# Cached attention on one core: transposing P on TensorE as 4-byte pairs of keys

## The chip, the cores and the metric

The kernel runs on one core of a Trainium2 chip. Time is the device time of one execution in microseconds (us). Before the change the median of two runs is 958.55 us (958.49 to 958.61).

## The reference

Two independent attention blocks, A and B, have the same shapes; their outputs are laid side by side. All tensors are bfloat16.

```python
B, Sq, D = 16, 64, 640
H, Sk, Dh = 32, 512, 128
q = (x @ wq).reshape(B, Sq, H, Dh).transpose(0, 2, 1, 3)
scores = jnp.einsum("bhqd,bhkd->bhqk", q, k_cache) * (Dh ** -0.5)
p = softmax(scores, axis=-1)
o = jnp.einsum("bhqk,bhkd->bhqd", p, v_cache)
return o.transpose(0, 2, 1, 3).reshape(B, Sq, H * Dh) @ wo
```

The K and V caches are most of the data: 16 x 32 x 512 x 128 elements each, for each block.

## The kernel before

**Tiling.** The 64 queries of two batch rows are put together to fill 128 partitions. A *step* g is one head of one such pair of batch rows; a *macro-step* m, called an iteration below, is two steps. A *group* is a pair of batch rows with 16 heads (8 iterations), a *pass* is half the heads of one block with all 8 pairs of batch rows. There are 4 passes and 256 iterations. K and V come in chunks of 4 heads through rings of five buffers, loaded on SyncE's queue (SP).

**One iteration**, by the names in the program (line numbers are those of the profile):

- KX (L433, TensorE) transposes K of the two heads, one batch row at a time (KX0, KX1: eight transposes of 128x128 each), into the one PSUM bank KTB. KE (L442, VectorE) copies the bank to `ktp_ring`. K is loaded with `t=8`: partition pp holds keys 8pp to 8pp+7, and so the transposed keys, and the scores after them, lie in the order (t, pp): key 8pp+t stands at place 64t+pp.
- QP2 (L451, TensorE) projects q, QE2 (L459, ScalarE) copies it out.
- SM2 (L467, TensorE) computes the scores of both steps into two PSUM banks, one for each step.
- MX (L476, VectorE) takes the row maximum; EX (L482, ScalarE) writes exp(score - max) to `p_ring` in bfloat16 and sums it to `rowsum`; RC2 (L488, VectorE) is the reciprocal of two sums.
- NM (L496, POOL) multiplies by the reciprocal and, with a permuting access pattern, writes `pn_ring` in the order in which the transposes need the keys.
- TR2 (L505, TensorE) transposes the normalised P: four 128x128 transposes for each step, eight in all, into the PSUM bank PTB; TE2 (L512, VectorE) copies the bank to `pT_ring`.
- PV2 (L524, TensorE) multiplies by V, which is loaded with `t=4` (partition p holds keys 4p to 4p+3); OE2 (L532, ScalarE) copies the result out.
- OP2 (L540, L545, TensorE) multiplies by wo and accumulates over the 16 heads of a group. At the group's end OVP (L555, ScalarE) stores a partial sum or, in the second pass of a block, OVF (L560, VectorE) adds it and writes `out_sb`, and ST sends that to DRAM from ScalarE's queue. XT (L604) and XE (L612) transpose x for a later group once in each group.

**Order.** Each engine runs a fixed list, made from templates that say which iteration (an offset to k) each operation works on in round k:

```python
PE_T = (("TR2", 1), ("QP2", 4), ("KX", 4, 0), ("SM2", 3), ("PV2", 1), ("XT", 0), ("OP2", 0), ("KX", 4, 1))
ACT_T = (("QE2", 4), ("OE2", 1), ("XE", 0), ("EX", 3, 0), ("EX", 3, 1), ("OV", 0), ("ST", -1))
DVE_T = (("TE2", 1), ("RC2", 2), ("KE", 4, 0), ("MX", 3, 0), ("MX", 3, 1), ("KE", 4, 1), ("OVF", 0))
POOL_T = (("NM", 0, 0), ("NM", 0, 1))
```

So a round on TensorE is TR2, QP2, KX0, SM2, PV2, OP2, KX1. Within an engine the order never changes. Between engines, `build_plan` lists the reads and writes of each operation, derives the dependences and turns them into semaphore waits. The loads on SP are sorted by due time from planned durations.

Of the kernel before, what the change touches and what calls it, by code (L numbers as in the profile page):

```python
# [64 lines left out]
def build_plan(dims, cfg):  # L65
# [32 lines left out]
    def make_op(kind, m, sub):  # L98
        g0, g1 = 2 * m, 2 * m + 1
        ps_, bp, grp, h0 = step_info(g0)  # L100
        c = g0 // G
        if kind == "KX":
            return mk("pe", "KX", (m, sub), [("kn", c % cfg.NKB, g0 % G), ("kn", c % cfg.NKB, g1 % G), ("ident",)],
                      [("KTB",)], "KX%d" % sub, m, sub)
        if kind == "KE":
            return mk("dve", "KE", (m, sub), [], [("KTB",), ("ktp", m % cfg.NKT, sub)], "KE%d" % sub, m, sub)
        if kind in ("MX", "EX", "NM"):
            g = 2 * m + sub
            r = g % cfg.NR
            if kind == "MX":  # L110
                return mk("dve", "MX", g, [], [("SB", sub), ("negmax", r)], "MX%d" % sub, m, sub)
            if kind == "EX":
                return mk("act", "EX", g, [("negmax", r)], [("SB", sub), ("p", g % cfg.NP), ("rowsum", r)],
                          "EX%d" % sub, m, sub)
            return mk("pool", "NM", g, [("p", g % cfg.NP), ("recip", r)], [("pn", g % cfg.NPN)], "NM%d" % sub, m, sub)
        r0, r1 = g0 % cfg.NR, g1 % cfg.NR
        if kind in ("XT", "XE"):
            mt = m + cfg.XLEAD
            if mt % MPG != 0 or not (0 <= mt < NMAC):
                return None  # L120
            gq = mt // MPG
            m_ts = mt - cfg.XLEAD + OFF["TR2"]
            if kind == "XT":
                return mk("pe", "XT", gq, [("xn", gq % cfg.NXN), ("ident",)], [("PTB",)], "XT", m_ts, aux=gq)
            return mk("act", "XE", gq, [], [("PTB",), ("xT", gq % cfg.NX)], "XE", m_ts, aux=gq)
        if kind == "QP2":
            return mk("pe", "QP2", m, [("xT", grp % cfg.NX), ("wq", ps_ % 2, h0 // G)], [("QB",)], "QP2", m)
        if kind == "QE2":
            return mk("act", "QE2", m, [], [("QB",), ("qT", m % cfg.NQ)], "QE2", m)
        if kind == "SM2":  # L130
            return mk("pe", "SM2", m, [("qT", m % cfg.NQ), ("ktp", m % cfg.NKT, 0), ("ktp", m % cfg.NKT, 1)],
                      [("SB", 0), ("SB", 1)], "SM2", m)
        if kind == "RC2":
            return mk("dve", "RC2", m, [("rowsum", r0), ("rowsum", r1)], [("recip", r0), ("recip", r1)], "RC2", m)
        if kind == "TR2":
            return mk("pe", "TR2", m, [("pn", g0 % cfg.NPN), ("pn", g1 % cfg.NPN), ("ident",)], [("PTB",)], "TR2", m)
        if kind == "TE2":
            return mk("dve", "TE2", m, [], [("PTB",), ("pT", m % cfg.NT)], "TE2", m)
        if kind == "PV2":
            return mk("pe", "PV2", m, [("pT", m % cfg.NT), ("v", c % cfg.NVB, g0 % G), ("v", c % cfg.NVB, g1 % G)],  # L140
                      [("OB",)], "PV2", m)
        if kind == "OE2":
            return mk("act", "OE2", m, [], [("OB",), ("oT", m % cfg.NO)], "OE2", m)
        if kind == "OP2":
            return mk("pe", "OP2", m, [("oT", m % cfg.NO), ("wo", ps_ % 2, h0 // G)], [("OUTB",)], "OP2", m)
        if kind in ("OV", "OVF", "ST"):
            if h0 + 1 != SPB - 1:
                return None
            last_half = ps_ % NHALF == NHALF - 1
            if kind == "OV":  # L150
                if NHALF == 1:
                    return mk("act", "OV", m, [], [("OUTB",), ("out_sb", grp % 2)], "OV", m, aux=grp)
                if last_half:
                    return None
                return mk("act", "OVP", m, [], [("OUTB",), ("outp", bp)], "OV", m, aux=grp)
            if kind == "OVF":
                if NHALF == 1 or not last_half:
                    return None
                return mk("dve", "OVF", m, [("outp", bp)], [("OUTB",), ("out_sb", grp % 2)], "OV", m, aux=grp)
            if NHALF == 1 or not last_half:  # L160
                return None
            return mk("act", "ST", m, [("out_sb", grp % 2)], [("out_dram", grp)], "ST", m, aux=grp)
        raise ValueError(kind)

    templates = {"pe": cfg.PE_T, "dve": cfg.DVE_T, "pool": cfg.POOL_T, "act": cfg.ACT_T}
    for eng, tmpl in templates.items():
        offs = [t[1] for t in tmpl] + [cfg.XLEAD]
        for k in range(-max(offs), NMAC - min(offs)):
            for t in tmpl:
# [8 lines left out]
                if 0 <= m < NMAC:  # L178
                    op = make_op(kind, m, sub)
                    if op is not None:  # L180
                        progs[eng].append(op)
                        if op.kind == "OV":
                            progs[eng].append(mk("act", "ST", m, [("out_sb", op.aux % 2)], [("out_dram", op.aux)],
                                                 "ST", m, aux=op.aux))

    progs["pool"] = [mk("pool", "INIT1", -1, [], [("ones",)], "LDW", -10),
                     mk("pool", "INIT2", -1, [("ones",)], [("ident",)], "LDX", -10)] + progs["pool"]

    loads = []
    NEG = -10 ** 9  # L190
# [53 lines left out]
    def sem_key(op):  # L244
# [5 lines left out]
            return ("d_" + op.kind[2:].lower(), op.aux[0] % 2, op.aux[1])  # L250
        if op.kind == "ST":
            return ("d_out", op.aux % 2)
        if op.kind in ("INIT1", "INIT2"):
            return ("s_init",)
        return ("s_" + op.kind.lower(),)

# [90 lines left out]
def mha_kernel(nc, blocks, out, cfg=None):  # L347
# [30 lines left out]
    with contextlib.ExitStack() as es:  # L378
# [13 lines left out]
        qT_ring = sb("qT_ring", [128, NQ, 2, 128], BF16)  # L392
        p_ring = sb("p_ring", [128, NP, SK], BF16)
        pn_ring = sb("pn_ring", [128, NPN, SK], BF16)
        pT_ring = sb("pT_ring", [128, NT, 2, 4, 128], BF16)
        oT_ring = sb("oT_ring", [128, NO, 2, 128], BF16)
        out_sb = sb("out_sb", [128, 2, DN], BF16)
        negmax = sb("negmax", [128, NR], F32)
        rowsum = sb("rowsum", [128, NR], F32)
        recip = sb("recip", [128, NR], F32)  # L400
        ones_sb = sb("ones_sb", [128, 128], BF16)
        ident = sb("ident", [128, 128], BF16)
        ps = es.enter_context(nc.psum_tensor("ps", [128, 8, 512], F32))

        sems = {}
# [9 lines left out]
        S_BANK0 = 2  # L415
        PT_BANK, O_BANK, Q_BANK, KT_BANK = 4, 5, 6, 7
        pt_ps_flat = ps[:, PT_BANK, :].bitcast(BF16)
        pt_ps = pt_ps_flat.rearrange("p (s t q) -> p s t q", s=2, t=4)
        o_ps = ps[:, O_BANK, 0:256]
        q_ps = ps[:, Q_BANK, 0:256]  # L420
        kt_ps_flat = ps[:, KT_BANK, :].bitcast(BF16)
# [57 lines left out]
        def em_EX(e, op):  # L479
            g = op.idx  # L480
            r = g % NR
            ins = e.activation(p_ring[:, g % NP, :], s_bank(g % 2), ACTF.Exp, bias=negmax[:, r:r + 1], scale=1.0,  # L482
                               accum_out=rowsum[:, r:r + 1])
            return ins, ins

# [5 lines left out]
        def em_NM(e, op):  # L491
            g = op.idx
            r = g % NR
            src = p_ring[:, g % NP, :].rearrange("q (th tl pp) -> q th tl pp", th=2, tl=4)
            dst = pn_ring[:, g % NPN, :].rearrange("q (tl pp th) -> q th tl pp", tl=4, th=2)
            ins = e.tensor_scalar(dst, src, recip[:, r:r + 1], 1.0, ALU.mult, ALU.mult)  # L496
            return ins, ins

        def em_TR2(e, op):
            m = op.idx  # L500
            first = last = None
            for sub in range(2):
                g = 2 * m + sub
                for t in range(4):
                    ins = e.transpose(pt_ps[:, sub, t, :], pn_ring[:, g % NPN, t * 128:(t + 1) * 128], ident[:, :])  # L505
                    first = first or ins
                    last = ins
            return first, last

        def em_TE2(e, op):  # L510
            m = op.idx
            ins = e.tensor_copy(pT_ring[:, m % NT].rearrange("p s t q -> p (s t q)"), pt_ps_flat)  # L512
            return ins, ins

        def em_PV2(e, op):
            m = op.idx
            first = last = None
            for sub in range(2):
                g = 2 * m + sub
                c, gi = g // G, g % G  # L520
                for j in range(2):
                    for t in range(4):
                        col = sub * 128 + 64 * j
                        ins = e.matmul(o_ps[:, col:col + 64], v_ring[:, c % NVB, j, gi, t, :],  # L524
                                       pT_ring[:, m % NT, sub, t, 64 * j:64 * j + 64], start=(t == 0), stop=(t == 3))
                        first = first or ins
                        last = ins
            return first, last
# [18 lines left out]
            return first, last  # L547

        def em_OV(e, op):
            ins = e.activation(out_sb[:, op.aux % 2, :], out_ps_all, ACTF.Copy)  # L550
            return ins, ins

        def em_OVP(e, op):
# [3 lines left out]

        def em_OVF(e, op):
            blk, bp = grp_info(op.aux)
            ins = e.tensor_tensor(out_sb[:, op.aux % 2, :], out_ps_all, outp[:, bp, :], ALU.add)  # L560
            return ins, ins

        def em_ST(e, op):
            blk, bp = grp_info(op.aux)
            dst = out[2 * bp:2 * bp + 2, :, blk * DN:(blk + 1) * DN].rearrange("b q n -> (b q) n")
            ins = e.dma_start(dst, out_sb[:, op.aux % 2, :])
            return ins, ins

        def em_INIT1(e, op):
# [2 lines left out]

        def em_INIT2(e, op):
            ins = e.affine_select(ident[:, :], ones_sb[:, :], [[1, 128]], ALU.is_equal, 0.0, base=0,
                                  channel_multiplier=-1)
            return ins, ins

# [38 lines left out]
        def em_LDKV(e, op):  # L616
# [6 lines left out]
            else:  # L623
# [4 lines left out]

        emitters = dict(KX=em_KX, KE=em_KE, QP2=em_QP2, QE2=em_QE2, SM2=em_SM2, MX=em_MX, EX=em_EX, RC2=em_RC2,
                        NM=em_NM, TR2=em_TR2, TE2=em_TE2, PV2=em_PV2, OE2=em_OE2, OP2=em_OP2, OV=em_OV,  # L630
                        OVP=em_OVP, OVF=em_OVF, ST=em_ST, XT=em_XT, XE=em_XE, INIT1=em_INIT1, INIT2=em_INIT2,
                        LDWQ=em_LDWQ, LDWO=em_LDWO, LDX=em_LDX, LDK=em_LDKV, LDV=em_LDKV)

        def run_program(e, prog, final_waits=()):
# [85 lines left out]
```

## Time and profile before

| What | Value |
|---|---|
| median of the runs | 958.55 us |
| profiled execution, span from first to last instruction | 956.8 us |
| TensorE busy | 919.4 us (96%) |
| VectorE busy | 841.9 us (88%) |
| ScalarE busy | 567.1 us (59%) |
| POOL busy | 416.9 us (44%) |
| DMA | 299.51 MB, mean 313 GB/s |
| mean granted TensorE clock | 0.998 |

The profiled execution is one of its own; its span is 1.75 us below the median of the timed runs. Busy time of TensorE counts each matmul with its latency, and neighbours overlap: the time of a burst is read from its first start to its last end, or from the chain of waits. In the groups of the page, the number after the busy time is the mean duration of one instruction in ns; what follows the second bar is the idle time of the engine just before the group's instructions, and what ended it. PEld are the weight loads of TensorE. In the timeline the columns are start, duration, engine, line, operation, output and inputs, and how many instructions are merged in the row.

### The profile page before, as it was taken

The numbers are of one execution on the slowest core, as the hardware profiler recorded it, in microseconds if no ns is written. First come the engines' busy times: TensorE is split into PE (matmuls) and PEld (weight loads), VectorE is DVE, ScalarE is ACT, GpSimd is POOL, SyncE is SP. The second block draws the span as 40 slices with busy tenths as digits, with TensorE's granted clock in tenths as the row PEclk, the third lists the DMA queues.
The fourth block names the chain that finished last, engine by engine and source line by source line (L and its number), as shares of the span: only waits on it lengthen the run. The fifth ranks groups of instructions, "written<-read, shape, count | busy, mean of one in ns | idle before, by whom it ended". The sixth has DMA issues, their size and how long they took to land.

```text
span 956.8 us, 34351 instructions
## 1 busy us (share of the span) xinstructions
PE 919.4 (96%) x14755; PEld 733.5 (77%) x15008; DVE 841.9 (88%) x1552; ACT 567.1 (59%) x1585; POOL 416.9 (44%) x518
## 2 busy tenths in 40 slices
PE   4999999999999999999999999999999999999997
PEld 3877777778777777877777787777877778777775
DVE  2898899898899999899999899889899998999996
ACT  1666656666665565656566666666666656565654
POOL 0444444444444444444444444444444444444443
PEclk9999999999999999999999999999999999999999
DMA  9999999999999999888999999988888988899830
GB/s 315 364 365 364 351 365 367 365 368 351 338 337 337 343 330 315 299 292 305 322 332 352 326 353 327 306 294 296 302 305 288 308 301 297 295 297 314 295 124 15
DMA packets 230871, 299.51 MB, mean 313 GB/s; under 512 B 9536, under 2 KB 165184, under 8 KB 230720
## 3 DMA queue, kind: packets, MB, share of 16 engines
q1 hardware_dynamic: 228416, 294.69, 91.0%
q8 instruction: 118, 1.93, 0.8%
q10 hardware_dynamic: 2304, 2.62, 0.8%
q14 instruction: 33, 0.27, 0.1%
HBM read 294.65 MB, written 2.62 MB: 311 GB/s over the span
## 4 chain that ended last, share of the span: by engine, by line
PE 89%; DVE 4%; POOL 3%; issue 2%; SPq 1%; DMA 1%; POOLq 0%; DVEq 0%
PE ps L433 22%; PE ps L524 14%; PE ps L451 14%; PE ps L467 14%; PE ps L505 12%; PE ps L545 7%; PE ps L540 5%; POOL pn_ring L496 3%; DVE out_sb L560 1%; DVE ktp_ring L442 1%; DVE pT_ring L512 1%; PE ps L604 1%; DMA xn_ring<-in_A_x_dram 1%; SPq L626 1%; SPq L583 1%
## 5 line engine op out<-in xcount | busy, mean ns | idle before, releaser
L496 POOL TENSOR_SCALAR pn_ring<-p_ring,recip 128x512 bf16<-128x512 bf16 x512 | 416.3, 843 | 532.7 <-DVE recip L488 532.7
L442 DVE COPY ktp_ring<-ps 128x1024 bf16<-128x1024 bf16 x512 | 353.7, 691 | 105.3 <-PE ps L433 85.1
L482 ACT ACTIVATE p_ring<-ps,negmax 128x512 bf16<-128x512 f32 x512 | 345.6, 684 | 4.8 <-DVE negmax L476 4.8
L476 DVE TENSOR_REDUCE negmax<-ps 128x1 f32<-128x512 f32 x512 | 327.3, 681 | 0.4 <-PE ps L467 0.3
L433 PE MATMUL ps<-ident,kn_ring 128*128 128x128 bf16 x4096 | 314.6, 220 | 2.8 <-DMA kn_ring<-in_A_k_cache_dram 1.6
L532 ACT ACTIVATE oT_ring<-ps 128x256 bf16<-128x256 f32 x256 | 98.0, 383 | 306.0 <-PE ps L524 306.0
L433 PEld LDWEIGHTS ps<-ident,kn_ring 128*128 128x128 bf16 x4096 | 251.9, 98 | 34.2 <-DVE ktp_ring L442 2.6
L524 PEld LDWEIGHTS ps<-pT_ring,v_ring 128*128 128x128 bf16 x4096 | 133.5, 98 | 109.2 <-issue 100.0
L451 PE MATMUL ps<-xT_ring,wq_sb 128*128 128x128 bf16 x2560 | 186.4, 220 | 3.2 <-DMA wq_sb<-in_A_wq_dram 3.2
L512 DVE COPY pT_ring<-ps 128x1024 bf16<-128x1024 bf16 x256 | 174.5, 682 | 4.6 <-PE ps L505 3.8
L524 PE MATMUL ps<-pT_ring,v_ring 128*128 128x64 bf16 x4096 | 163.8, 194 | 3.3 <-issue 1.7
L467 PE MATMUL ps<-ktp_ring,qT_ring 128*64 128x512 bf16 x1024 | 159.8, 392 | 0.4 <-ACT p_ring L482 0.4
L505 PE MATMUL ps<-ident,pn_ring 128*128 128x128 bf16 x2048 | 156.7, 219 | 3.5 <-POOL pn_ring L496 3.5
L451 PEld LDWEIGHTS ps<-xT_ring,wq_sb 128*128 128x128 bf16 x2560 | 155.2, 98 | 3.5 <-DMA wq_sb<-in_A_wq_dram 3.5
L459 ACT ACTIVATE qT_ring<-ps 128x256 bf16<-128x256 f32 x256 | 98.4, 384 | 66.8 <-PE ps L451 66.8
L505 PEld LDWEIGHTS ps<-ident,pn_ring 128*128 128x128 bf16 x2048 | 124.1, 98 | 7.0 <-POOL pn_ring L496 6.7
L545 PE MATMUL ps<-wo_sb,oT_ring 128*128 128x128 bf16 x512 | 112.1, 219 | 13.4
L482 ACT ACTIVATION_READ_ACCUMULATOR p_ring<-ps,negmax 128x1 f32 x512 | 105.0, 205 | 0.0
L540 PE MATMUL ps<-wo_sb,oT_ring 128*128 128x512 bf16 x259 | 97.8, 379 | 0.0
L540 PEld LDWEIGHTS ps<-wo_sb,oT_ring 128*128 128x128 bf16 x512 | 50.1, 98 | 30.6 <-ACT oT_ring L532 0.3
L467 PEld LDWEIGHTS ps<-ktp_ring,qT_ring 128*64 128x64 bf16 x1024 | 36.1, 108 | 27.1 <-ACT p_ring L482 0.6
L545 PEld LDWEIGHTS ps<-wo_sb,oT_ring 128*128 128x128 bf16 x512 | 50.1, 98 | 0.0
(13 smaller groups left out, 112.7 us busy)
## 6 DMA issues: line engine op xcount, KB each, us to landing
kn_ring<-in_A_k_cache_dram SPq DMA_DIRECT2D x128, 512.0 KB, 7.0
v_ring<-in_A_v_cache_dram SPq DMA_DIRECT2D x128, 512.0 KB, 7.2
kn_ring<-in_B_k_cache_dram SPq DMA_DIRECT2D x126, 512.0 KB, 4.8
v_ring<-in_B_v_cache_dram SPq DMA_DIRECT2D x126, 512.0 KB, 5.7
wq_sb<-in_A_wq_dram SPq DMA_DIRECT2D x8, 640.0 KB, 10.4
wo_sb<-in_A_wo_dram SPq DMA_DIRECT2D x8, 640.0 KB, 10.2
wq_sb<-in_B_wq_dram SPq DMA_DIRECT2D x8, 640.0 KB, 8.4
wo_sb<-in_B_wo_dram SPq DMA_DIRECT2D x8, 640.0 KB, 7.5
```

The source lines that it names most:

```text
L433: ins = e.transpose(kt_ps[:, t8, :], kn_ring[:, c % NKB, j, hp, t8, :], ident[:, :])
L442: ins = e.tensor_copy(dst, src)
L451: ins = e.matmul(q_ps[:, sub * 128:(sub + 1) * 128], wq_sb[:, ps_ % 2, kt, hh * DH:(hh + 1) * DH], xT_ring[:, grp % NX, kt, :], start=(kt ...
L467: ins = e.matmul(s_bank(sub)[64 * j:64 * j + 64, :], qT_ring[:, m % NQ, sub, 64 * j:64 * j + 64], ktp_ring[:, m % NKT, sub, j, :], start=T ...
L476: ins = e.reduce_max(negmax[:, r:r + 1], s_bank(g % 2), axis=AX.X, negate=True)
L482: ins = e.activation(p_ring[:, g % NP, :], s_bank(g % 2), ACTF.Exp, bias=negmax[:, r:r + 1], scale=1.0, accum_out=rowsum[:, r:r + 1])
L496: ins = e.tensor_scalar(dst, src, recip[:, r:r + 1], 1.0, ALU.mult, ALU.mult)
L505: ins = e.transpose(pt_ps[:, sub, t, :], pn_ring[:, g % NPN, t * 128:(t + 1) * 128], ident[:, :])
L512: ins = e.tensor_copy(pT_ring[:, m % NT].rearrange("p s t q -> p (s t q)"), pt_ps_flat)
L524: ins = e.matmul(o_ps[:, col:col + 64], v_ring[:, c % NVB, j, gi, t, :], pT_ring[:, m % NT, sub, t, 64 * j:64 * j + 64], start=(t == 0), s ...
L540: ins = e.matmul(out_ps0, oT_ring[:, m % NO, sub, :], wo_sb[:, ps_ % 2, hh, 0:N0], start=(hh == 0), stop=(hh == SPB - 1))
L545: last = e.matmul(out_ps1, oT_ring[:, m % NO, sub, :], wo_sb[:, ps_ % 2, hh, N0:DN], start=(hh == 0), stop=(hh == SPB - 1))
```

## The change

P is transposed in units of 4 bytes. Two neighbouring bfloat16 keys are taken as one 32-bit element: the step's 512 keys are 256 pairs, and transposes of 128x128 pairs, two for each step and four for each iteration, take the place of eight. Pair 2i+u goes to partition i, so that partition i receives keys 4i to 4i+3, which is how V is loaded; PV2 picks one key of a pair by reading `pT_ring` with a step of two elements. For this P must be in the natural order of keys: EX now writes `p_ring` with the permutation (steps of 8 elements between neighbours), and NM is a plain multiplication, contiguous on both sides. A 32-bit identity is made at the start (INIT3, INIT4). `out_sb` has one buffer in place of two.

```diff
-            return mk("pe", "TR2", m, [("pn", g0 % cfg.NPN), ("pn", g1 % cfg.NPN), ("ident",)], [("PTB",)], "TR2", m)
+            return mk("pe", "TR2", m, [("pn", g0 % cfg.NPN), ("pn", g1 % cfg.NPN), ("ident_f",)], [("PTB",)], "TR2", m)
...
-                return mk("dve", "OVF", m, [("outp", bp)], [("OUTB",), ("out_sb", grp % 2)], "OV", m, aux=grp)
+                return mk("dve", "OVF", m, [("outp", bp)], [("OUTB",), ("out_sb", 0)], "OV", m, aux=grp)
...
     progs["pool"] = [mk("pool", "INIT1", -1, [], [("ones",)], "LDW", -10),
-                     mk("pool", "INIT2", -1, [("ones",)], [("ident",)], "LDX", -10)] + progs["pool"]
+                     mk("pool", "INIT2", -1, [("ones",)], [("ident",)], "LDX", -10),
+                     mk("pool", "INIT3", -1, [], [("ones_f",)], "LDW", -9),
+                     mk("pool", "INIT4", -1, [("ones_f",)], [("ident_f",)], "LDX", -9)] + progs["pool"]
...
-        pT_ring = sb("pT_ring", [128, NT, 2, 4, 128], BF16)
+        pT_ring = sb("pT_ring", [128, NT, 2, 2, 128, 2], BF16)
...
-        out_sb = sb("out_sb", [128, 2, DN], BF16)
+        out_sb = sb("out_sb", [128, 1, DN], BF16)
...
+        ones_f = sb("ones_f", [128, 128], F32)
+        ident_f = sb("ident_f", [128, 128], F32)
...
-        pt_ps = pt_ps_flat.rearrange("p (s t q) -> p s t q", s=2, t=4)
+        ptf_ps = ps[:, PT_BANK, :].rearrange("p (s u q) -> p s u q", s=2, u=2)
...
         def em_EX(e, op):
             g = op.idx
             r = g % NR
-            ins = e.activation(p_ring[:, g % NP, :], s_bank(g % 2), ACTF.Exp, bias=negmax[:, r:r + 1], scale=1.0,
+            dst = p_ring[:, g % NP, :].rearrange("q (pp t) -> q t pp", t=8)
+            src = s_bank(g % 2).rearrange("q (t pp) -> q t pp", t=8)
+            ins = e.activation(dst, src, ACTF.Exp, bias=negmax[:, r:r + 1], scale=1.0,
                                accum_out=rowsum[:, r:r + 1])
...
-            src = p_ring[:, g % NP, :].rearrange("q (th tl pp) -> q th tl pp", th=2, tl=4)
-            dst = pn_ring[:, g % NPN, :].rearrange("q (tl pp th) -> q th tl pp", tl=4, th=2)
-            ins = e.tensor_scalar(dst, src, recip[:, r:r + 1], 1.0, ALU.mult, ALU.mult)
+            ins = e.tensor_scalar(pn_ring[:, g % NPN, :], p_ring[:, g % NP, :], recip[:, r:r + 1], 1.0, ALU.mult, ALU.mult)
...
                 g = 2 * m + sub
-                for t in range(4):
-                    ins = e.transpose(pt_ps[:, sub, t, :], pn_ring[:, g % NPN, t * 128:(t + 1) * 128], ident[:, :])
+                pn = pn_ring[:, g % NPN, :].bitcast(F32).rearrange("q (i u) -> q u i", u=2)
+                for u in range(2):
+                    ins = e.transpose(ptf_ps[:, sub, u, :], pn[:, u, :], ident_f[:, :])
...
         def em_TE2(e, op):
             m = op.idx
-            ins = e.tensor_copy(pT_ring[:, m % NT].rearrange("p s t q -> p (s t q)"), pt_ps_flat)
+            ins = e.tensor_copy(pT_ring[:, m % NT].rearrange("p s u q e -> p (s u q e)"), pt_ps_flat)
...
                         ins = e.matmul(o_ps[:, col:col + 64], v_ring[:, c % NVB, j, gi, t, :],
-                                       pT_ring[:, m % NT, sub, t, 64 * j:64 * j + 64], start=(t == 0), stop=(t == 3))
+                                       pT_ring[:, m % NT, sub, t // 2, 64 * j:64 * j + 64, t % 2], start=(t == 0), stop=(t == 3))
```

The other lines of the diff put `out_sb[:, 0, :]` in OV, OVF and ST, and add the two functions of INIT3 and INIT4 (a memset of `ones_f` to 1.0 and an affine_select into `ident_f`, as INIT1 and INIT2 do for `ident`).

More of the change, by code (lines that the diff above doesn't have):

```diff
@@ L151, in make_op @@
                 if NHALF == 1:
-                    return mk("act", "OV", m, [], [("OUTB",), ("out_sb", grp % 2)], "OV", m, aux=grp)
+                    return mk("act", "OV", m, [], [("OUTB",), ("out_sb", 0)], "OV", m, aux=grp)
                 if last_half:
@@ L158, in make_op @@
                     return None
-                return mk("dve", "OVF", m, [("outp", bp)], [("OUTB",), ("out_sb", grp % 2)], "OV", m, aux=grp)
+                return mk("dve", "OVF", m, [("outp", bp)], [("OUTB",), ("out_sb", 0)], "OV", m, aux=grp)
             if NHALF == 1 or not last_half:
                 return None
-            return mk("act", "ST", m, [("out_sb", grp % 2)], [("out_dram", grp)], "ST", m, aux=grp)
+            return mk("act", "ST", m, [("out_sb", 0)], [("out_dram", grp)], "ST", m, aux=grp)
         raise ValueError(kind)
@@ L182, in build_plan @@
                         if op.kind == "OV":
-                            progs[eng].append(mk("act", "ST", m, [("out_sb", op.aux % 2)], [("out_dram", op.aux)],
+                            progs[eng].append(mk("act", "ST", m, [("out_sb", 0)], [("out_dram", op.aux)],
                                                  "ST", m, aux=op.aux))
     progs["pool"] = [mk("pool", "INIT1", -1, [], [("ones",)], "LDW", -10),
-                     mk("pool", "INIT2", -1, [("ones",)], [("ident",)], "LDX", -10)] + progs["pool"]
+                     mk("pool", "INIT2", -1, [("ones",)], [("ident",)], "LDX", -10),
+                     mk("pool", "INIT3", -1, [], [("ones_f",)], "LDW", -9),
+                     mk("pool", "INIT4", -1, [("ones_f",)], [("ident_f",)], "LDX", -9)] + progs["pool"]
     loads = []
@@ L252, in sem_key @@
             return ("d_out", op.aux % 2)
-        if op.kind in ("INIT1", "INIT2"):
+        if op.kind in ("INIT1", "INIT2", "INIT3", "INIT4"):
             return ("s_init",)
@@ L549, in em_OV @@
         def em_OV(e, op):
-            ins = e.activation(out_sb[:, op.aux % 2, :], out_ps_all, ACTF.Copy)
+            ins = e.activation(out_sb[:, 0, :], out_ps_all, ACTF.Copy)
             return ins, ins
@@ L559, in em_OVF @@
             blk, bp = grp_info(op.aux)
-            ins = e.tensor_tensor(out_sb[:, op.aux % 2, :], out_ps_all, outp[:, bp, :], ALU.add)
+            ins = e.tensor_tensor(out_sb[:, 0, :], out_ps_all, outp[:, bp, :], ALU.add)
             return ins, ins
@@ L565, in em_ST @@
             dst = out[2 * bp:2 * bp + 2, :, blk * DN:(blk + 1) * DN].rearrange("b q n -> (b q) n")
-            ins = e.dma_start(dst, out_sb[:, op.aux % 2, :])
+            ins = e.dma_start(dst, out_sb[:, 0, :])
             return ins, ins
@@ L574, in em_INIT2, with em_INIT3, em_INIT4 @@
             ins = e.affine_select(ident[:, :], ones_sb[:, :], [[1, 128]], ALU.is_equal, 0.0, base=0,
+                                  channel_multiplier=-1)
+            return ins, ins
+        def em_INIT3(e, op):
+            ins = e.memset(ones_f[:, :], 1.0)
+            return ins, ins
+        def em_INIT4(e, op):
+            ins = e.affine_select(ident_f[:, :], ones_f[:, :], [[1, 128]], ALU.is_equal, 0.0, base=0,
                                   channel_multiplier=-1)
@@ L630, in mha_kernel @@
                         NM=em_NM, TR2=em_TR2, TE2=em_TE2, PV2=em_PV2, OE2=em_OE2, OP2=em_OP2, OV=em_OV,
-                        OVP=em_OVP, OVF=em_OVF, ST=em_ST, XT=em_XT, XE=em_XE, INIT1=em_INIT1, INIT2=em_INIT2,
+                        OVP=em_OVP, OVF=em_OVF, ST=em_ST, XT=em_XT, XE=em_XE, INIT1=em_INIT1, INIT2=em_INIT2, INIT3=em_INIT3, INIT4=em_INIT4,
                         LDWQ=em_LDWQ, LDWO=em_LDWO, LDX=em_LDX, LDK=em_LDKV, LDV=em_LDKV)
```

## The prediction

> **What bounds the kernel now.** I read the page first (busy shares, costliest groups), then the chain of waits inside the steady middle, then the timeline of one iteration. The page:
>
> ```profile
> span 956.8 us, 34351 instructions
> PE 919.4 (96%) x14755; PEld 733.5 (77%) x15008; DVE 841.9 (88%) x1552; ACT 567.1 (59%) x1585; POOL 416.9 (44%) x518
> ...
> L496 POOL TENSOR_SCALAR pn_ring<-p_ring,recip 128x512 bf16<-128x512 bf16 x512 | 416.3, 843 | 532.7 <-DVE recip L488 532.7
> ...
> L482 ACT ACTIVATE p_ring<-ps,negmax 128x512 bf16<-128x512 f32 x512 | 345.6, 684 | 4.8 <-DVE negmax L476 4.8
> ...
> L505 PE MATMUL ps<-ident,pn_ring 128*128 128x128 bf16 x2048 | 156.7, 219 | 3.5 <-POOL pn_ring L496 3.5
> ```
>
> TensorE is busy 96% of the span and VectorE 88%. The 219 ns of a transpose (L505) is its latency: the transposes overlap, and what counts is the step from one start to the next. The chain of waits between 400 and 420 us shows the steps as the path sees them, for one whole iteration (two heads of two batch rows):
>
> ```profile
> 412.93 0.45 PE ps L433 x8
> 413.38 0.45 PE ps L505 x8
> 413.82 0.56 PE ps L451 x10
> 414.38 0.45 PE ps L433 x8
> 414.83 0.55 PE ps L467 x4
> 415.38 0.57 PE ps L524 x16
> 415.95 0.05 issue
> 416.01 0.22 PE ps L545
> 416.23 0.21 PE ps L540
> 416.44 0.06 PE ps L545
> 416.50 0.45 PE ps L433 x8
> ```
>
> The path is TensorE alone, in the order KX1 (L433), TR2 (L505), QP2 (L451), KX0 (L433), SM2 (L467), PV2 (L524), OP2 (L540, L545), and round again after 416.50 - 412.93 = 3.57 us. There are 256 iterations: 256 x 3.57 = 914 us; the other 43 us are the start, the end and the group boundaries. The change works on TR2, 0.45 us of the 3.57. Whether a shorter TR2 shortens the round is read from the timeline, which shows what else goes on between KX1 and the next KX0:
>
> ```profile
> 100.34 0.49 PEld L433 LDWEIGHTS ps<-ident,kn_ring 128*128 128x128 bf16 x8
> ...
> 100.78 0.49 PEld L505 LDWEIGHTS ps<-ident,pn_ring 128*128 128x128 bf16 x8
> ...
> 101.04 0.69 DVE L442 COPY ktp_ring<-ps 128x1024 bf16<-128x1024 bf16 x1 [0.23 <-PE ps L433]
> 101.23 0.60 PEld L451 LDWEIGHTS ps<-xT_ring,wq_sb 128*128 128x128 bf16 x10
> ...
> 101.79 0.49 PEld L433 LDWEIGHTS ps<-ident,kn_ring 128*128 128x128 bf16 x8
> ```
>
> Both KX0 and KX1 write the one bank KTB, and KE (L442, VectorE) must empty it between them. KX1 starts at 100.34, KE1 waits for it until 101.04 and ends at 101.73, and KX0 starts at 101.79. **That is 0.06 us after KE1 ends.** Pair by pair over the trace the gap from the end of KE1 to KX0 has a median of 58 ns, and its shortest value, 53 ns, is that of a KX0 that really waits for KE1 (at the start of the run). So KX0 has some 5 ns to spare. Two ways from KX1 to KX0 are equally long: KX1, TR2, QP2 on TensorE (0.45 + 0.45 + 0.56 = 1.46 us) and KX1's completion, KE1, semaphore (0.70 + 0.69 + 0.05 = 1.44 us). Only the first contains TR2.
>
> **The change, part by part.**
>
> *TR2, eight transposes become four of 4-byte elements.* Today's price: the timeline gives eight transposes 0.61 us from first start to last end; less 0.219 for the last, 0.39 over 7 steps is 56 ns a step, 8 x 56 = 0.45 us. No 4-byte operand of TensorE is in this trace, so the new step x is bounded. Low end: x = 56 ns, the same 128 columns at the same rate; TR2 = 0.22 us. High end: no overlap at all, weight load plus matmul, 98 + 219 = 317 ns; TR2 = 1.27 us. Between them: 112 ns if the time goes with the bytes, which makes TR2 just what it was; 149 ns if each load is exposed like the one at KX0 to SM2 (first KX0 matmul 101.84, eighth 7 x 0.056 later at 102.23, first SM2 matmul 102.38: 0.15 us where a step is 0.056); 219 ns if each transpose runs by itself. The nearest row is L505 itself, of the same shape and with twice the bytes in each element, so I take x between 56 and 112 ns, TR2 between 0.22 and 0.45 us.
>
> What TR2 saves there is up to 0.22 us of TensorE time in an iteration, **and I cost it at almost nothing**: the next thing late is KX0, which meets KE1. The other way round stays 0.70 + 0.69 + 0.05 to KX0, then KX0, SM2, PV2, OP2 as before. The round can lose the spare 5 ns, 256 x 0.005 = 1.3 us. If that cover were gone, a TR2 of 0.22 would be worth 0.225 x 256 = 58 us. In the other direction nothing hides it: above 112 ns each further ns of x costs 4 x 256 ns = 1.02 us.
>
> [...]
>
> *EX writes natural order, in steps of 8 elements (16 bytes).* 684 ns now, contiguous. ScalarE's price of an element is (702 - 383)/(640 - 256) = 0.83 ns, from the xT copy (L612) and the qT copy (L459). Bounds: nothing, or a doubled element price, 512 x 0.83 = 0.425 us for each EX, 0.85 us for the pair. The nearest row with a permuted write is KE, 691 ns in runs of 64, against TE2's contiguous 682 for as many elements: 9 ns. I take nothing. What hides small growth: EX1's accumulator read starts at 101.56 and the SM2 that needs its bank starts at 102.38, 0.82 us later, of which 0.26 is the read and the semaphore: 0.56 us to spare. RECIPROCAL, queued on VectorE ahead of KE0 and both MX, has 0.33.
>
> [...]
>
> *NM reads and writes contiguously.* 843 ns now, with 4-byte steps in its write. It can stay or shorten; I see no reason for it to grow. It waits for RECIPROCAL nearly always and TR2 starts 0.23 us after it ends where 0.05 would do, so in the steady round it is worth nothing. It counts at the 16 boundaries where OVF (L560, 0.815 us) delays RECIPROCAL: the two rounds there are 3.75 and 3.90 us, together 0.51 us long: at most 16 x 0.51 = 8.2 us for NM and TR2 together. I take half of TR2's largest saving, 16 x 0.11 = 1.8 us.
>
> *PV2 reads P transposed with a step of two elements.* Step now: (0.64 - 0.193)/15 = 30 ns. No strided matmul operand is in the trace: nothing, or a doubled step, 16 x 30 = 0.48 us an iteration. The nearest row is PV2 itself with as many columns: nothing.
>
> *Hidden parts.* TE2 copies the same bytes, 682 ns. INIT3 and INIT4 stand behind INIT1 and INIT2 (0.20 and 0.29 us) on POOL, which is then idle for 17 us until the first NM; only if that cover failed would they cost their own 1 us. One out_sb in place of two makes OVF wait for the previous store, 5.6 us to landing, issued a group (8 x 3.57 = 28.5 us) earlier; were it late, TE2, RECIPROCAL and KE0 stand behind OVF on VectorE. No load is moved in any queue.
>
> Sum, against the profiled span: 956.8 - 1.3 - 1.8 = 953.7 us. The timed runs stand 1.75 us above the span (958.55), so 955.5; I say 956.
>
> **The rivals.**
>
> *The 4-byte transposes are dear (slower).* One mechanism: on TensorE between KX1 and QP2, price (4x - 0.446) x 256, deciding from x = 112 ns, and over 2% (19 us) from 131 ns. At 149 ns: 0.15 x 256 = 38 us, 997 us. At 219 ns: 0.43 x 256 = 110 us, 1069 us. At 317 ns: 210 us, 1169 us. For it: no row shows such an operand, and TensorE has no idle time to give. Against: the columns are halved. Halving the instruction count without halving the work would be this case too: the change would then not do what it says.
>
> *EX binds.* A doubled element price is 0.85 us against 0.56 to spare: 0.29 x 256 = 74 us, 1033 us. For: no element would lie beside the last one written. Against: ACT is 59% busy.
>
> *PV2's read doubles.* 0.48 x 256 = 123 us, 1081 us. For: TensorE sets the path there. Against: half of each touched stretch is still used.
>
> *Faster by over 2%.* The 58 us of a fourfold 56 ns would give 901 us, if KX0 were not held by KE1; VectorE's own work in a round is 3.34 us (3.57 less its one idle 0.23), so it would have room. Against it stands the single bank, and those 5 ns.
>
> **How the numbers follow.** A measurement of this kernel tells about 2% from no change. Chances: no change as worked out 0.48; dear transposes 0.35, of which 0.02 stay within 2%; EX 0.07; PV2 0.07; faster 0.03. So within 2% is 0.50, slower 0.47, faster 0.03. The likeliest single case gives 956 us, and its own range is 948 (all 8.2 us of the boundaries, and the 1.3) to 965. The other cases hold half the chance, so the range must reach to them: to 1076 it takes in the dear transposes up to 219 ns and EX; left out are most of PV2, the unpipelined 317 ns and the faster case, under 0.15 together.
>
> **What the changed profile would show.** If I am right: 1,024 transposes, their step at 112 ns or under; PEld of KX waiting for DVE ktp_ring for up to 0.22 x 256 = 57 us in place of 2.6; PE busy down; a round still 3.56 us; EX within 0.28 us of 684 ns; PV2 still 0.64 us for 16. If the transposes are dear, the chain shows TR2 over 0.45 us, KX0 starts long after KE1 ends, and PE stays on the chain throughout. If EX binds, SM2 or RECIPROCAL waits for ACT in every round. A KX0 that starts earlier than 1.44 us after KX1 would overturn the argument itself.

## The result and the profile after: 1773.89 us, 1.851 times the time before

The changed kernel takes 1773.89 us (1773.57 to 1774.21, two runs) against 958.55 us: a ratio of 1.851, 95% interval 1.846 to 1.856. The time lies far outside the forecast range, and the part that set it is the one that the prediction gave a chance of 0.07: EX.

The page of the changed kernel (busy us, share, instructions; then granted TensorE clock in tenths; the chain; groups):

```profile
span 1772.4 us, 32305 instructions
...
PE 1105.4 (62%) x13731; PEld 846.2 (48%) x13984; DVE 855.5 (48%) x1552; ACT 1392.3 (79%) x1585; POOL 349.0 (20%) x520
...
PEclk8989998888998889988898988989889888888888
...
ACT 73%; PE 23%; issue 2%; SPq 1%; DMA 0%; POOL 0%; DVE 0%; POOLq 0%; DVEq 0%
...
L488 ACT ACTIVATE p_ring<-ps,negmax 128x512 bf16<-128x512 f32 x512 | 1233.8, 2655 | 1.8 <-DVE negmax L480 1.8
L500 POOL TENSOR_SCALAR pn_ring<-p_ring,recip 128x512 bf16<-128x512 bf16 x512 | 347.8, 692 | 1414.9 <-DVE recip L494 1414.9
...
L510 PEld LDWEIGHTS ps<-ident_f,pn_ring 128*128 128x128 f32 x1024 | 146.0, 210 | 4.1 <-POOL pn_ring L500 3.6
```

EX (L488 here) went from 684 to 2655 ns; ScalarE is now 73% of the chain, TensorE 23%. NM (L500) became shorter, 692 ns for 843. A weight load of TR2 (L510) takes 210 ns where it took 98, by this row of the kernel before:

```profile
L505 PEld LDWEIGHTS ps<-ident,pn_ring 128*128 128x128 bf16 x2048 | 124.1, 98 | 7.0 <-POOL pn_ring L496 6.7
```

And the granted clock of TensorE, 0.998 before, is 0.88 on average.

ScalarE in one round of the timeline:

```profile
501.70 2.55 ACT L488 ACTIVATE p_ring<-ps,negmax 128x512 bf16<-128x512 f32 x1
503.74 0.51 ACT L488 ACTIVATION_READ_ACCUMULATOR p_ring<-ps,negmax 128x1 f32 x1
503.76 2.75 ACT L488 ACTIVATE p_ring<-ps,negmax 128x512 bf16<-128x512 f32 x1
506.01 0.50 ACT L488 ACTIVATION_READ_ACCUMULATOR p_ring<-ps,negmax 128x1 f32 x1
```

The same two EX in the kernel before, and the SM2 that waits for the bank of the second:

```profile
100.33 0.68 ACT L482 ACTIVATE p_ring<-ps,negmax 128x512 bf16<-128x512 f32 x1
...
100.99 0.69 ACT L482 ACTIVATE p_ring<-ps,negmax 128x512 bf16<-128x512 f32 x1
...
102.38 0.62 PE L467 MATMUL ps<-ktp_ring,qT_ring 128*64 128x512 bf16 x4
```

Durations overlap; the better measure is from start to start: 503.76 - 501.70 = 2.06 us, where it was 100.99 - 100.33 = 0.66 us. The median over all pairs is 2.07 us. This spacing is used below as "the EX spacing".

What that does to the round is read from the chain of waits between 501 and 516 us:

```profile
501.80 4.73 ACT p_ring L488 x4
506.53 0.04 issue
506.57 0.62 PE ps L471 x4
507.19 0.60 PE ps L529 x16
507.79 0.02 issue
507.81 0.38 ACT oT_ring L537
508.20 4.73 ACT p_ring L488 x4
512.93 0.04 issue
512.97 1.07 PE ps L471 x4
514.03 0.97 PE ps L529 x16
```

SM2 (L471) waits for EX1 to free its bank, in 255 of the 256 rounds:

```profile
PE ps L471 <- ACT p_ring L488: 617.8, 255, 3.0
```

(The numbers are the total wait in us, how often, and the longest.) PV2 (L529) is queued behind SM2 on TensorE. OE2 (L537), which waits for PV2, stands before the next EX on ScalarE. So EX, SM2, PV2 and OE2 now follow one another: 4.73 + 0.04 + 0.62 + 0.60 + 0.02 + 0.38 = 6.39 us in place of 3.57. ScalarE is itself idle in that loop, 1.09 us before the OE2 at 507.81; no run moves OE2 behind EX. In the second of these rounds SM2 takes 1.07 and PV2 0.97 us. The table by stretches shows why (stretch, its length, busy us of PE, PEld, DVE, ACT and POOL, granted clock, DMA share, GB/s):

```profile
504.00:508.00 4.00, 1.90 (x32) 1.23 (x31) 1.75 (x5) 2.91 (x6) 1.19 (x2) 1.00 0.52 176
508.00:512.00 4.00, 2.31 (x33) 2.02 (x30) 1.81 (x3) 4.00 (x4) 0.17 (x1) 1.00 0.50 164
512.00:516.00 4.00, 2.81 (x27) 1.95 (x29) 2.04 (x4) 1.94 (x5) 1.36 (x2) 0.59 0.27 102
```

In the stretch from 512 us, in which TensorE comes back from a wait for EX, the granted clock is 0.59, and the matmuls on the path take 0.8 us more in that round. It isn't so after every wait: SM2 takes its 0.62 us in 151 of the 256 rounds, and about 1.07 us in the other 105.

### The profile page after: what moved, and what is told of

Same layout as the page of the kernel before. It is cut to its first block, busy times and chain, and to the rows that moved or that the text cites. A ratio compares the mean times of both kernels' runs of the same rounds, so it can differ in the third digit from the quotient of the medians.

```text
span 1772.4 us, 32305 instructions
## 1 busy us (share of the span) xinstructions
PE 1105.4 (62%) x13731; PEld 846.2 (48%) x13984; DVE 855.5 (48%) x1552; ACT 1392.3 (79%) x1585; POOL 349.0 (20%) x520
## 4 chain that ended last, share of the span: by engine, by line
ACT 73%; PE 23%; issue 2%; SPq 1%; DMA 0%; POOL 0%; DVE 0%; POOLq 0%; DVEq 0%
ACT p_ring L488 67%; PE ps L471 11%; PE ps L529 11%; ACT oT_ring L537 5%; ACT xT_ring L626 1%; PE ps L618 1%; DMA xn_ring<-in_A_x_dram 0%; SPq L640 0%; SPq L597 0%; SPq L636 0%; POOL pn_ring L500 0%; PE ps L545 0%; DVE out_sb L565 0%; PE ps L510 0%; POOLq L380 0%
## 5 line engine op out<-in xcount | busy, mean ns | idle before, releaser
L488 ACT ACTIVATE p_ring<-ps,negmax 128x512 bf16<-128x512 f32 x512 | 1233.8, 2655 | 1.8 <-DVE negmax L480 1.8
L500 POOL TENSOR_SCALAR pn_ring<-p_ring,recip 128x512 bf16<-128x512 bf16 x512 | 347.8, 692 | 1414.9 <-DVE recip L494 1414.9
L471 PE MATMUL ps<-ktp_ring,qT_ring 128*64 128x512 bf16 x1024 | 205.8, 491 | 617.8 <-ACT p_ring L488 617.8
L537 ACT ACTIVATE oT_ring<-ps 128x256 bf16<-128x256 f32 x256 | 98.4, 384 | 357.6 <-PE ps L529 357.6
L494 DVE RECIPROCAL recip<-rowsum 128x2 f32<-128x2 f32 x256 | 42.5, 166 | 670.5 <-ACT p_ring L488 670.5
L471 PEld LDWEIGHTS ps<-ktp_ring,qT_ring 128*64 128x64 bf16 x1024 | 40.6, 121 | 662.4 <-ACT p_ring L488 662.2
L488 ACT ACTIVATION_READ_ACCUMULATOR p_ring<-ps,negmax 128x1 f32 x512 | 261.7, 511 | 0.0
L529 PEld LDWEIGHTS ps<-pT_ring,v_ring 128*128 128x128 bf16 x4096 | 172.7, 110 | 148.4 <-issue 148.4
L529 PE MATMUL ps<-pT_ring,v_ring 128*128 128x64 bf16 x4096 | 207.3, 213 | 1.7 <-issue 1.7
L510 PE MATMUL ps<-ident_f,pn_ring 128*128 128x128 f32 x1024 | 184.2, 304 | 3.3 <-POOL pn_ring L500 3.3
L463 ACT ACTIVATE qT_ring<-ps 128x256 bf16<-128x256 f32 x256 | 173.9, 679 | 8.5 <-PE ps L455 8.5
L510 PEld LDWEIGHTS ps<-ident_f,pn_ring 128*128 128x128 f32 x1024 | 146.0, 210 | 4.1 <-POOL pn_ring L500 3.6
L545 PEld LDWEIGHTS ps<-wo_sb,oT_ring 128*128 128x128 bf16 x512 | 59.3, 116 | 47.3 <-issue 29.2
```

The source lines that it names most:

```text
L471: ins = e.matmul(s_bank(sub)[64 * j:64 * j + 64, :], qT_ring[:, m % NQ, sub, 64 * j:64 * j + 64], ktp_ring[:, m % NKT, sub, j, :], start=T ...
L488: ins = e.activation(dst, src, ACTF.Exp, bias=negmax[:, r:r + 1], scale=1.0, accum_out=rowsum[:, r:r + 1])
L500: ins = e.tensor_scalar(pn_ring[:, g % NPN, :], p_ring[:, g % NP, :], recip[:, r:r + 1], 1.0, ALU.mult, ALU.mult)
L510: ins = e.transpose(ptf_ps[:, sub, u, :], pn[:, u, :], ident_f[:, :])
L537: ins = e.activation(oT_ring[:, m % NO].rearrange("p s q -> p (s q)"), o_ps, ACTF.Copy)
L545: ins = e.matmul(out_ps0, oT_ring[:, m % NO, sub, :], wo_sb[:, ps_ % 2, hh, 0:N0], start=(hh == 0), stop=(hh == SPB - 1))
```

## The experiments

### One part undone, one part alone

The changed kernel with EX contiguous (e1):

```diff
-            dst = p_ring[:, g % NP, :].rearrange("q (pp t) -> q t pp", t=8)
-            src = s_bank(g % 2).rearrange("q (t pp) -> q t pp", t=8)
-            ins = e.activation(dst, src, ACTF.Exp, ...
+            ins = e.activation(p_ring[:, g % NP, :], s_bank(g % 2), ACTF.Exp, ...
```

> The changed kernel with EX writing contiguously again, everything else as changed (keys then meet the wrong V rows: the permutation of P is left out). Theory A, EX's stepped write is the whole loss: EX back to 0.68 us, time 958 to 968 us; the 4-byte transposes at the 118 ns step seen in the changed kernel cost (4 x 118 - 446) ns x 256 = 7 us, and NM's 692 ns in place of 843 can give back up to 8 us. Rival B, the 4-byte transposes and the lower TensorE clock carry a good part of it: EX at 0.68 us but over 985 us. If transposes of 4-byte pairs gained as halved work would, TR2 under 0.30 us.

Measured: 979.13 us, ratio 1.022 (1.020 to 1.023).

```profile
L486 ACT ACTIVATE p_ring<-ps,negmax 128x512 bf16<-128x512 f32 x512 | 345.6, 684 | 4.6 <-DVE negmax L480 4.6
```

Theory A is right about EX, 684 ns, but 11 us short: the transposes cost more than the 7 us that their step promised. The chain of this kernel between 500 and 520 us (KX1, TR2, QP2):

```profile
511.73 0.45 PE ps L437 x8
512.17 0.54 PE ps L508 x4
512.71 0.56 PE ps L455 x10
```

TR2 (L508) is 0.54 us, not 0.45; over the trace the median round is 3.667 us, not 3.567. The 100 ns are 26 us over 256 rounds; 5 us come back at the 16 boundaries with OVF, where two rounds of 3.75 and 3.90 us became two of 3.76, since NM is shorter.

The kernel before, with EX's stepped write alone (e2; NM then regroups P on its reading side, as the diff shows):

```diff
+            dst = p_ring[:, g % NP, :].rearrange("q (pp t) -> q t pp", t=8)
+            src = s_bank(g % 2).rearrange("q (t pp) -> q t pp", t=8)
...
-            src = p_ring[:, g % NP, :].rearrange("q (th tl pp) -> q th tl pp", th=2, tl=4)
-            dst = pn_ring[:, g % NPN, :].rearrange("q (tl pp th) -> q th tl pp", tl=4, th=2)
+            src = p_ring[:, g % NP, :].rearrange("q (i tl) -> q tl i", tl=4)
+            dst = pn_ring[:, g % NPN, :].rearrange("q (tl i) -> q tl i", tl=4)
```

> The kernel before with one part of the change alone: EX writes natural key order (16-byte steps) and NM reads it with a step of four elements; eight 2-byte transposes as before. Theory A: EX 2.6 us, time 1740 to 1800 us as in the changed kernel, granted clock about 0.88. Rival B: below 1600 us, the rest being due to the 4-byte transposes.

Measured: 1772.79 us (one run), EX 2647 ns, mean clock 0.871. The stepped write, with the lower clock that comes with it, makes the whole loss; under it, the dearer transposes are hidden.

### What about the write is dear

Five kernels differ from the changed one only in how EX writes or reads, one run each. In e3, e4 and e10 the `t=8` of EX is 2, 4 and 64:

> The changed kernel with EX writing in steps of 2 elements (4 bytes) in place of 8 (the permutation of P is only partly done). If the price is that of leaving a 16-byte stretch with every element (four elements fall into one here): EX near 0.68 us and 955 to 975 us. Rival, any write that is not contiguous pays in full: EX 2.6 us, about 1770 us. Third, the price grows with the step: EX 0.8 to 1.5 us, 970 to 1250 us.

> The changed kernel with EX writing in steps of 4 elements (8 bytes; the permutation of P is only partly done). 16-byte stretches, two elements in each: EX near 0.68 us, 955 to 975 us. Any stepped write pays in full: EX 2.6 us, about 1770 us. Price in proportion to the step: EX about 1.3 us, some 1100 to 1300 us.

> The changed kernel with EX writing in steps of 64 elements (128 bytes) in place of 8 (the permutation of P is another one). From contiguous to 2, 4 and 8 elements EX starts came 0.66, 0.77, 1.19 and 2.07 us apart. If the price stops growing once every element lies in a 16-byte stretch of its own: 2.07 us again and about 1770 us. If it grows with the distance: over 4 us and over 2500 us.

| EX writes | EX, mean ns | EX spacing, us | time, us |
|---|---|---|---|
| contiguous (e1) | 684 | 0.66 | 979.13 |
| steps of 2 elements (e3) | 841 | 0.77 | 979.07 |
| steps of 4 (e4) | 1413 | 1.19 | 1118.51 |
| steps of 8 (changed kernel) | 2655 | 2.07 | 1773.89 |
| steps of 64 (e10) | 2672 | 2.08 | 1774.53 |

For e3 and e4 the third theory holds, a price that grows with the step; for e3 it is EX's 841 ns that says so, for its time is that of the contiguous EX. e10 shows that the price stops growing at 16 bytes or before 128. Step 2 costs no time, because the pair of EX grows by less than the 0.56 us that the prediction found to spare.

The same permutation on the reading side (e5):

```diff
-            dst = p_ring[:, g % NP, :].rearrange("q (pp t) -> q t pp", t=8)
-            src = s_bank(g % 2).rearrange("q (t pp) -> q t pp", t=8)
+            dst = p_ring[:, g % NP, :].rearrange("q (pp t) -> q pp t", t=8)
+            src = s_bank(g % 2).rearrange("q (t pp) -> q pp t", t=8)
```

> The changed kernel, the same permutation made on EX's reading side: EX reads the scores from PSUM in steps of 64 elements (256 bytes) and writes P contiguously in natural order. If the price is one of writing in steps: EX 0.68 us, about 979 us as with the contiguous EX. If ScalarE pays for any operand that is not contiguous: EX 2.6 us or more, about 1770 us or more. Between: each read costs something of its own, EX 0.8 to 1.5 us.

Measured: 979.28 us (one run). The page of this kernel:

```profile
span 977.5 us, 32305 instructions
...
L488 ACT ACTIVATE p_ring<-ps,negmax 128x512 bf16<-128x512 f32 x512 | 345.6, 684 | 4.4 <-DVE negmax L480 4.4
```

Reading PSUM in steps of 256 bytes costs ScalarE nothing here: 684 ns, to the nanosecond what the contiguous EX takes, with the same natural order in `p_ring`. The price belongs to the write.

The last one writes two neighbours at a time (e16):

```diff
+            dst = p_ring[:, g % NP, :].rearrange("q (pp h e) -> q h pp e", h=4, e=2)
+            src = s_bank(g % 2).rearrange("q (h e pp) -> q h pp e", h=4, e=2)
```

> The changed kernel with EX's natural order written two neighbours at a time: two adjacent elements, then 16 bytes on (the scores are read in steps of 64 for that). EX starts 0.77, 1.19, 2.07 us apart for steps of 2, 4, 8 elements fit 0.32 us + 3.4 ns for each change from one 16-byte stretch to another (128, 256, 512 changes). If that is the price: 256 changes, 1.19 us, and about 1118 us as with steps of 4. If each element that is not followed in one run costs by itself: 2.07 us and about 1770 us; if only the distance of 16 bytes between runs counts little: 0.66 us and about 979 us.

Measured: 977.86 us (one run), EX spacing 0.685 us.

```profile
L488 ACT ACTIVATE p_ring<-ps,negmax 128x512 bf16<-128x512 f32 x512 | 361.4, 723 | 4.5 <-DVE negmax L480 4.5
```

My price for each change of a 16-byte stretch is refuted: this kernel makes as many changes as e4, and takes 0.69 us where e4 takes 1.19. The third possibility is the nearest: the distance between the runs of two counts little. In these kernels what is dear is an element written without an adjacent partner, and dearer the farther the next one is, up to 16 bytes (0.77, 1.19 and 2.07 us at 4, 8 and 16 bytes). What in the chip makes it so, no run here tells.

### The clock

The changed kernel with more K transposes for TensorE while it waits (e7):

```diff
-            for t8 in range(8):
+            for t8 in [i % 8 for i in range(8 if j else 32)]:
```

> The changed kernel with 32 K transposes in KX0 in place of 8 (the same eight written four times), 1.34 us more TensorE work in each round, in the time in which TensorE waits for EX. If the low granted clock during those waits is part of the loss: granted clock up from 0.88 to over 0.97 and time down from 1774 us to 1650 to 1720 us (256 rounds of 4.73 + 0.04 + 0.62 + 0.60 + 0.02 + 0.38 = 6.39 us are 1636 us). Rival, the clock doesn't matter since ScalarE sets the round: 1760 to 1790 us or more.

Measured: 1691.26 us (one run), 83 us less than the changed kernel, with 1.34 us more work for TensorE in every round. Its page:

```profile
span 1689.5 us, 44593 instructions
...
PEclk9999999999999999999999999999999999999999
```

EX is unchanged (2667 ns), the mean clock is 0.998, and no other part was touched. SM2 takes 0.62 us in all rounds but one, where in the changed kernel 105 rounds were some 0.83 us longer from SM2 to OE2: 105 x 0.83 = 87 us. So about 83 of the 815 us lost are the low clock after TensorE's waits; the rest stays. What lets the clock fall after some waits and not after others is not shown.

### Is KX0 held by KE1?

The central claim of the prediction was that a shorter TR2 is worth almost nothing. It is tested on the kernel before (e6):

```diff
-                for t in range(4):
+                for t in range(4 if m < 2 else 2):
                     ins = e.transpose(pt_ps[:, sub, t, :], ...
```

> The kernel before with four 2-byte transposes in TR2 in place of eight from the third iteration on (half of P transposed is left out), so that TR2 is what four transposes at the 56 ns step would be, 0.22 us. The prediction's theory (KX0 is held by KE1 through the one bank KTB): the round stays at 3.56 us, time 948 to 957 us, and KX's weight loads wait for KE some 50 us in total. Rival (TensorE's busy time sets the round): 0.22 x 256 = 57 us less, 895 to 910 us.

Measured: 945.51 us, ratio 0.987 (0.985 to 0.989): 13 us of the 57 us that were cut from TensorE, a little below the theory's range and far above the rival's. The waits, and then the timeline of one round (KE1, then KX0's loads and matmuls):

```profile
PEld ps L433 <- DVE ktp_ring L442: 43.7, 239, 1.1
```

```profile
501.27 0.69 DVE L442 COPY ktp_ring<-ps 128x1024 bf16<-128x1024 bf16 x1 [0.23 <-PE ps L433]
...
502.02 0.45 PEld L433 LDWEIGHTS ps<-ident,kn_ring 128*128 128x128 bf16 x8 [0.18 <-DVE ktp_ring L442]
502.02 0.62 PE L433 MATMUL ps<-ident,kn_ring 128*128 128x128 bf16 x8
```

KX0 now waits for KE1 in 239 rounds, 53 ns after KE1's end, as claimed. But the median round fell from 3.567 to 3.523 us, 44 ns and not 5. Before, KX0's first load started at 101.79 and its first matmul at 101.84; here both start at 502.02. The first load was issued ahead and its 50 ns lay before the matmul; when the load waits, they are gone. Over the trace KX0's first matmul comes 55 ns sooner after KX1's, and KX0's own eight then take 10 ns longer, which leaves the 44. The prediction had counted the spare time to the load, not to the matmul.

### Why four 4-byte transposes cost more than eight

In the changed kernel a transpose takes every second pair, so that the operand it loads lies in steps of 8 bytes. Here (e12), with EX on the reading side, it takes 128 adjacent pairs, so that the kernel leaves out part of the permutation:

```diff
-                pn = pn_ring[:, g % NPN, :].bitcast(F32).rearrange("q (i u) -> q u i", u=2)
+                pn = pn_ring[:, g % NPN, :].bitcast(F32).rearrange("q (u i) -> q u i", u=2)
```

> The changed kernel with EX permuting on its reading side, and the 4-byte transposes reading 128 adjacent pairs in place of every second pair (the pairs then meet the wrong V rows). If the step of two pairs makes the 4-byte loads slow: TR2 0.25 to 0.35 us on the chain and the round back at 3.52 to 3.57 us, 945 to 958 us. If 4-byte elements cost this in any order: TR2 0.54 us, round 3.66 us, 976 to 982 us.

Measured: 957.16 us, ratio 0.9984 (0.9975 to 0.9993). Its chain (KX1, TR2, QP2) and its loads:

```profile
501.55 0.45 PE ps L437 x8
502.00 0.44 PE ps L510 x4
502.44 0.56 PE ps L455 x10
```

```profile
L510 PEld LDWEIGHTS ps<-ident_f,pn_ring 128*128 128x128 f32 x1024 | 107.9, 141 | 2.3 <-POOL pn_ring L500 1.2 <-ACT xT_ring L626 0.2
```

The time came out as expected for slow loads, though not by the TR2 that I had written beside it: 0.44 us, not 0.25 to 0.35. The load falls from 210 to 141 ns, and the three steps of a TR2 are 116, 109 and 109 ns (medians); with every second pair they are 170, 125 and 120. So there are two separate facts: a 4-byte transpose takes twice the step of a 2-byte one (109 against 56 ns), which makes four as long as eight (0.443 us from TR2 to QP2 against 0.447); and taking every second pair costs another 0.09 us in a round, 22 us in all (979.28 - 957.16).

### Versions without the losses

The whole change with both losses mended (e15): EX on the reading side, NM regrouping P so that a transpose finds adjacent pairs.

```diff
+            src = p_ring[:, g % NP, :].rearrange("q (i u e) -> q u i e", u=2, e=2)
+            dst = pn_ring[:, g % NPN, :].rearrange("q (u i e) -> q u i e", u=2, e=2)
```

> The 4-byte transposes with both losses taken out and the whole permutation done: EX permutes on its reading side, NM writes P so that the 128 pairs of a transpose are adjacent (reading with a step of two pairs), the transposes read adjacent pairs. Theory: EX 0.68 us, TR2 0.44 us on the chain, round 3.57 us: 953 to 960 us, like the version with adjacent pairs that left the order out, and not below the 2-byte version with EX on the reading side (954.75 us). Rival: NM's regrouping makes POOL late (over 1.0 us each) and TR2 waits for it: 965 us or more.

Measured: 956.96 us, ratio 0.9982 (0.9972 to 0.9991). NM takes 692 ns with this regrouping. And the 2-byte transposes with the other half of the change (e11), EX on the reading side and a contiguous NM:

```diff
+                pn = pn_ring[:, g % NPN, :].rearrange("q (i t) -> q t i", t=4)
                 for t in range(4):
-                    ins = e.transpose(pt_ps[:, sub, t, :], pn_ring[:, g % NPN, t * 128:(t + 1) * 128], ident[:, :])
+                    ins = e.transpose(pt_ps[:, sub, t, :], pn[:, t, :], ident[:, :])
```

> The kernel before with three edits: EX permutes on its reading side (PSUM steps of 64 elements, contiguous write in natural order), NM is contiguous, and the eight 2-byte transposes take their operand from natural order in steps of four elements (8 bytes). Theory: EX 0.68 us as on the reading side before, NM 0.69 us in place of 0.84, TensorE's round unchanged at 3.57 us; the 16 boundaries where OVF holds up RECIPROCAL and NM give back up to 0.3 us each: 953 to 957 us. Rival: a stationary operand in steps of 8 bytes loads more slowly: TR2 0.55 us or more on the chain, 975 us or more.

Measured: 954.75 us, ratio 0.9955 (0.9941 to 0.9968), the fastest version. Its page:

```profile
L496 POOL TENSOR_SCALAR pn_ring<-p_ring,recip 128x512 bf16<-128x512 bf16 x512 | 349.4, 695 | 595.1 <-DVE recip L490 595.1
...
L506 PEld LDWEIGHTS ps<-ident,pn_ring 128*128 128x128 bf16 x2048 | 128.2, 114 | 2.5 <-POOL pn_ring L496 1.3
```

The median round is 3.567 us as before. At the 16 boundaries with OVF the second round fell from 3.901 to 3.656 us: 16 x 0.245 = 3.9 us, the whole gain. A 2-byte operand in steps of 8 bytes loads in 114 ns instead of 98, and the steps, 56 ns as before, hide it. Everything else mended alike, the 4-byte transposes thus gain nothing over the 2-byte ones: 0.9982 of the time before against 0.9955, with intervals that do not meet, and a round of 3.574 us against 3.567.

## Why the prediction was wrong

**The step that failed is the price of EX's stepped write.** The sum took it at nothing, and its bounds, "nothing, or a doubled element price", had no row behind the upper end: the nearest row, KE's write in runs of 64, is not like single elements 16 bytes apart. The EX spacing rose by 1.41 us, where the doubled price was 0.425. The rival that EX binds had named the circumstance that then proved dear, that no element would lie beside the last one written, but the size that it put beside it was the doubled bound again, and the chance 0.07. What that rival says of the round, that EX holds up SM2, came true, and its arithmetic holds with the right price. From EX0's start to the SM2 that it frees took 2.05 us (100.33 to 102.38), 0.56 of it to spare, so 1.49 us were needed; now 4.87 are (501.70 to 506.57). That is 3.38 us more, less the 0.56 to spare 2.82 us a round, which is also what the chain shows (6.39 - 3.57). 2.82 x 256 = 722 us on 958.55 are 1681 us; the kernel with the clock at 0.998 (e7) takes 1691.

**A loss that was not on the list:** the clock. The prediction took TensorE's rates as fixed. Once TensorE waits for EX in 255 of the 256 rounds, they are not: the granted clock is 0.88 on average in place of 0.998, and SM2 takes about 1.07 us in place of 0.62 in 105 rounds: 83 us.

**Sum of the loss, from the runs,** one part taken off after another: clock 1774 - 1691 = 83; EX's write 1691 - 979 = 712; every second pair 979 - 957 = 22; together 817, and 957 stands 2 below the kernel before. The order matters: with the stepped write in place the 22 us are hidden, and e2 is as slow without them.

**TR2.** The chosen 56 to 112 ns held the 4-byte transpose itself (109 ns, adjacent pairs). As the change writes it, TR2 is 0.54 us, which is 135 ns each by the prediction's formula and above the chosen range: that the loaded operand lies in steps of two pairs had no price there. (0.54 - 0.446) x 256 = 24 us, against 22 measured. The break-even of 112 ns and the 2% mark at 131 ns fit the runs: this kernel without EX's loss stands at 2.2%, some 5 us of NM's gain at the boundaries included. The prediction's account of PV2 holds too: 16 matmuls in 0.65 us in the changed kernel at full clock, as before 0.64.

**KX0 held by KE1.** Right in kind and shown, but 44 ns a round could be lost and not 5. **Boundaries:** taken as 1.8 us from TR2, with nothing from NM; in fact NM gave them, 4 to 5 us. **Hidden parts:** the new identity, the single out_sb and TE2 (681 ns) show no cost in any run.

**The range** was the larger fault: a cost that no row of the trace resembles was given a ceiling of twice, and 0.07. With no such row the ceiling should have been left open, and the range with it.

## What to carry to other kernels

When a permutation must be put somewhere, try each side of each engine that touches the data: here it cost nothing on ScalarE's reading side (EX 684 ns, as without it) and nearly all of the 815 us, directly and through the clock, on its writing side (EX 2655 ns). Before counting instructions saved, ask what one of the new ones takes: half as many transposes of twice the bytes were no shorter (0.443 us against 0.447). And a bound for an operand pattern that the trace does not contain must not be taken from one that merely has the same size.

## What was not expected of the hardware

- ScalarE, writing 2-byte elements singly: 0.77, 1.19, 2.07 and 2.08 us between two EX of 512 elements in steps of 4, 8, 16 and 128 bytes, 0.66 contiguous, but 0.69 for two neighbours in every 16 bytes. Its read of PSUM in steps of 256 bytes is free (684 ns in both orders).
- In the changed kernel the accumulator read after EX takes 511 ns, where it took 205, and the copy that follows EX1 (QE2) 679 ns, where it took 384.
- TensorE's granted clock falls to 0.59 in a stretch of 4 us, with no wait for EX longer than 3.2 us, and 1.34 us of useless transposes in each round bring it back to 0.998 and the kernel 83 us forward.
- A stationary operand (the one that a weight load brings in) in steps of 8 bytes takes 210 against 141 ns a load with 4-byte elements, and 114 against 98 with 2-byte elements.
